# A planned kernel on one core: the planner's prices for turns between tile modes, 110 priorities and the lateness of one state update are changed

## The chip, the core and the metric

The kernel runs on 1 core of one Trainium2 chip. The metric is the device time of a run in microseconds (us); smaller is better. An engine is named as the profile names it where its lines are quoted: PE is TensorE, DVE VectorE, ACT ScalarE, POOL GpSimd, SP the engine that issues most DMAs here.

## What is computed

Two steps follow each other. The first is a gated linear attention, a recurrence over 768 tokens for each of 4 x 8 (batch, head) pairs of width 48:

```python
for t in range(S):
    state = alpha[:, :, t, :, None] * state + einsum('bhd,bhe->bhde', k[:, :, t], v[:, :, t])
    y[:, :, t] = einsum('bhd,bhde->bhe', q[:, :, t], state)
```

The second takes y as 3072 tokens of 384 features through two dense layers with a squared ReLU between them:

```python
h = x @ w_in            # 384 -> 2048, "first layer"
r = maximum(h, 0.0)
return (r * r) @ w_out  # 2048 -> 384, "second layer"
```

All inputs are float32; the kernel multiplies in bfloat16 and adds up in float32.

## The kernel before

**Units.** The work is cut into 12 units of 256 tokens of one batch entry (`units`, line 359; first the first 256 tokens of each of the 4 entries, so units 0 to 3 start a sequence, 4 to 7 continue it, 8 to 11 end it). For a unit there are

- four loads of 384 KB (`ld` a, k, q, v for alpha, k, q, v; `load`, line 494). The loads of unit 2 are issued by GpSimd, all others by SP;
- a front part (`front`, `decays_by_pair`): products of pairs of alphas (`pr`), logarithms (`ln`, `lm`), sums of them on TensorE (`m1i`, `m1s`, the decay sums), exponentials (`ei`, `ea`, `es`, `ec`), then k and q times those (`ekm`, `eqm0`, `eqm1`, lines 687 and 692). From unit 3 on, two DMA transposes (`tr0`, `tr1`, line 703) put the products into the layout for the scores; before that TensorE transposes;
- scores (`p0`, line 881), 32 matmuls on 64x64 tiles into the PSUM tensors psX and psZ, and two masks on VectorE (`mk0` reads psX, `mk1` psZ, line 892) that copy them to SBUF;
- the output (`y`, lines 773 and 784, or 813 and 820), matmuls on 64-row tiles into psX, with the matmuls of the next unit's state update (`kv`, line 752, into psZ) within it from unit 2 on. For units 0 to 2 the update's matmuls are an operation of their own. `sa`, `sc`, `sd` (lines 847 to 858) finish the state on VectorE or GpSimd;
- the eviction of the output (`xe`), its transposition (`xt`, by TensorE at line 927 up to unit 3, by DMA at line 933 after), and for TensorE's a copy (`xv`);
- the first layer in 8 pieces `s1_unit_piece` of 6 matmuls each (line 983), each evicted with a ReLU (`re`, ScalarE line 991 or VectorE line 993) and squared (`sq`);
- the second layer in 8 pieces `s2_unit_half_piece` of 4 matmuls (line 1018), evicted by `oe`, and one store (`out`, line 1034).

The weights are loaded in halves by GpSimd (`win0`, `win1`, `wout0`, `wout1`, line 480).

**The planner.** No order is written out by hand. Every operation is added with an engine (some with a choice of two or three), an assumed cost, a priority and its dependencies (`add`, line 58). `schedule` (line 101) then plays the whole program through with the assumed costs: whenever an engine is free, it takes the ready operation of the smallest priority number. What comes out is a fixed order for each engine (and the engine of each operation with a choice); `place` and `emit` turn dependencies into semaphore waits. So the assumed costs take no time on the chip; they only shape the order. An operation of TensorE has a mode: F for full 128x128 tiles (both layers, decay sums, transposes), T for the scores' 64x64 tiles, R and C for the outputs and updates. A change of mode is called a turn here. `schedule` charges 95 ns for a turn (`SWITCH`, line 45), and stays in a mode while an operation of that mode is ready whose priority number is at most 2500 above the best (`AFFINITY`, line 185).

Priorities come from the unit's number and tables at the head of the kernel function (`FRONT`, `ATTN`, `DENSE`). `LATE_STATE` names units whose state update is added with 4300 instead of 2300 on its priority (line 839), and whose mask of psZ is put before that of psX (line 890).

Until the first weights are there, TensorE is kept busy by matmuls on zeros (`fill`, line 213, called at line 1068).

Of the kernel before, what the change touches and what calls it, by code (L numbers as in the profile page):

```python
# [14 lines left out]
class Op:  # L15
# [5 lines left out]
    def __init__(self, alts, prio, name):  # L21
        self.alts, self.prio, self.name = alts, prio, name
        self.eng = self.fn = self.cost = None
        self.deps = {}
        self.lag = 0
        self.sem = None
        self.users = []
        self.pos = None
        self.mode = ("F", "F")
        self.ready = 0.0  # L30
        self.start = self.end = self.land = None


class Program:
# [7 lines left out]
    SBUF_ONLY = ("pr", "bk", "aq", "ekm", "eqm", "sq", "sb", "sd")  # L42
    BIAS = {"pool": 300}
    DMA_LAST = 800
    SWITCH = 95
    HALVED = {"qks": 3, "kqt": 3, "raw": 3, "ek": 3, "eq": 3, "acm": 2, "laf": 2}
    AFFINITY = 2500

    def __init__(self, nc):
        self.nc = nc  # L50
# [7 lines left out]
    def add(self, eng, fn, cost, prio, reads=(), writes=(), name="", dma=None, lag=0, after=(), mode=("F", "F"),  # L58
            alts=None):

        reads, writes = ([h for k in keys for h in ((k + (0,), k + (1,)) if len(k) == self.HALVED.get(k[0]) else (k,))]
                         for keys in (reads, writes))
        choices = {eng: (fn, cost)}
        if alts:
            choices.update(alts)
        op = Op(choices, prio, name)
        op.idx = len(self.ops)
        op.lag = lag
        op.mode = mode
        if dma is not None:  # L70
            if dma not in self.dma_sems:
                self.dma_sems[dma] = self.nc.alloc_semaphore("d_" + dma)
                self.dma_count[dma] = 0
            self.dma_count[dma] += 1
            op.sem = (dma, self.dma_count[dma])
        for o in after:
            op.deps[o] = True
        for k in reads:
            w = self.writer.get(k)
            if w is not None:  # L80
                op.deps[w] = True
            if k[0] == "ps":
                for r in self.readers.get(k, ()):
                    op.deps.setdefault(r, False)
        for k in writes:
            w = self.writer.get(k)
            if w is not None:
                op.deps[w] = True
            for r in self.readers.get(k, ()):
                if r is not op:  # L90
                    op.deps.setdefault(r, False)
        for k in reads:
            self.readers.setdefault(k, []).append(op)
        for k in writes:
            self.writer[k] = op
            self.readers[k] = []
        op.deps.pop(op, None)
        self.ops.append(op)
        return op

    def schedule(self):
# [8 lines left out]
        mode = "F"  # L110
# [6 lines left out]
        def push(t, kind, what):  # L117
            heapq.heappush(events, (t, next(seq), kind, what))
# [40 lines left out]
        avail = {e: [] for e in engines}  # L159
        order = {e: [] for e in engines}  # L160
        while events:
            now = events[0][0]
            while events and events[0][0] <= now + 1e-9:
                _, _, kind, op = heapq.heappop(events)
                if kind == "tick":
                    if op == clock[1]:
                        advance(now)
                elif kind == "arrive":
                    advance(now)
                    rings[op.eng].append(op)  # L170
                    left[op] = op.lag
                    advance(now)
                elif kind == "ready":
                    best = None
                    for e, (_, c) in op.alts.items():
                        t = max(now, free[e]) + c + self.BIAS.get(e, 0)
                        t += sum(o.alts[e][1] for o in avail[e] if (o.prio, o.idx) < (op.prio, op.idx))
                        if best is None or t < best[0]:
                            best = (t, e)
                    avail[best[1]].append(op)  # L180
            for e in engines:
                while avail[e] and free[e] <= now + 1e-9:
                    o = min(avail[e], key=lambda o: (o.prio, o.idx))
                    if e == "pe" and o.mode[0] != mode:
                        same = [x for x in avail[e] if x.mode[0] == mode and x.prio <= o.prio + self.AFFINITY]
                        if same:
                            o = min(same, key=lambda o: (o.prio, o.idx))
                    avail[e].remove(o)
                    o.eng = e
                    o.fn, o.cost = o.alts[e]  # L190
                    o.start = now
                    o.end = now + o.cost
                    if e == "pe":
                        if o.mode[0] != mode:
                            o.end += self.SWITCH
                        mode = o.mode[1]
                    if e == "pool" or e == "dve" and o.name.startswith(self.SBUF_ONLY):
                        other = shared["dve" if e == "pool" else "pool"]
                        o.end += max(0.0, min(other - now, 1200.0)) * (0.8 if e == "dve" else 0.5)
                        shared[e] = o.end  # L200
                    free[e] = o.end
                    o.pos = len(order[e])
                    order[e].append(o)
                    if o.sem is not None:
                        push(o.end + self.DMA_FIRST[e], "arrive", o)
                    else:
                        land(o, o.end + (self.PE_LATENCY if e == "pe" else 0))
                    push(free[e], "free", None)
# [130 lines left out]
def bass_gla_recurrent__then__act_relu_squared_kernel(  # L339
# [13 lines left out]
    T = 256  # L353
# [12 lines left out]
    RATIO = 4  # L366
    NRAW, NQKS, NKQT, NPM, NV, NXT, NGT, NRR, NOSB = 4, 3, 3, 2, 4, 4, 2, 4, 2
    WS = 2
    LATE_STATE = (1, 2)
    ROW_TILED = tuple(range(PE_TRANSPOSED, G))  # L370
    BY_HEADS = (0,)
    LAST_CUT = 272
# [48 lines left out]
    def table(act):  # L421
# [3 lines left out]
        return None  # L425

    add("act", table, 1300, -1e6, name="table")

    def fill(buf, val):
# [32 lines left out]
    def bcast(t, row, dims):  # L462
        return bass.AP(tensor=t, offset=0, ap=[[row, 128]] + dims)
# [367 lines left out]
    def state(g, alone=True):  # L831
# [5 lines left out]
        if alone:  # L837
            run, cost, reads, writes = state_mm(g)
            add("pe", run, cost, p0 + (4300 if g in LATE_STATE else 2300), reads=reads, writes=writes, name=f"kv{g}", mode=("R", "R"))
        own = bcast(OWN, H, [[1, H], [0, D]])  # L840
# [19 lines left out]
    def scores(g):  # L860
# [24 lines left out]
        for hfs in ((0,), (1,)) if g in BY_HEADS else ((0, 1),):  # L885
# [3 lines left out]
                mode=("T", "T"))  # L889
        for at, hf in enumerate((1, 0) if g in LATE_STATE else (0, 1)):  # L890
            psT, key = halves[hf]
# [208 lines left out]
```

## Time and profile before

| what | us |
|---|---|
| median of 3 runs (lowest, highest) | 176.63 (176.28, 177.08) |
| span of the profiled execution, first to last instruction | 174.5 |
| TensorE busy | 167.6 (96%) |
| VectorE busy | 121.7 (70%) |
| ScalarE busy | 118.9 (68%) |
| GpSimd busy | 15.3 (9%) |

The page gives the profiled execution by its span alone; the 2.1 us between span and median lie before the first and behind the last instruction. The granted TensorE clock is full throughout. The largest groups on TensorE are the first layer (576 matmuls of 256 columns at line 983, busy 73.6) and the second (368 of 384 columns at line 1018, busy 69.4). Matmuls overlap, so busy times of single matmuls add up to more than the time that passes; where pieces are compared below, the time from the start of one to the start of the next is used. A line of the timeline gives the start, the length, the engine, the source line, the operation with its output and inputs, how many were merged, and in brackets how long the engine stood idle before and what ended that. "PEld" is TensorE's loading of weights, beside its matmuls.

### The profile page before, as it was taken

What the parts mean: (1) busy time and instruction counts of PE and PEld (TensorE: products, weight loads), DVE (VectorE), ACT (ScalarE), POOL (GpSimd) and SP (SyncE); (2) the same over time, 40 slices, a digit from 0 to 9 for tenths busy, and PEclk for the clock granted to TensorE, in tenths of its full rate; (3) what the DMA queues carried; (4) which work ended last, traced back from release to release, by engine and by line L of the source; (5) the groups of instructions that cost most, each with busy time, mean ns of one, the idle gap of its engine ahead of it and who ended that gap; (6) DMA issues with size and microseconds to landing.
All of it is one profiled execution on the core that took longest, in us unless ns stands there. A gap on an engine that the chain in (4) does not pass through costs nothing.

```text
span 174.5 us, 5086 instructions
## 1 busy us (share of the span) xinstructions
PE 167.6 (96%) x2233; PEld 129.9 (74%) x2235; DVE 121.7 (70%) x201; ACT 118.9 (68%) x211; POOL 15.3 (9%) x24
## 2 busy tenths in 40 slices
PE   7998988999999989999999999999999999999994
PEld 2566887856787669778778878878788797688773
DVE  5597959596958599978869958958769726322230
ACT  3863689777769669578679759669578564566440
POOL 3160840020002002000200000000000000000000
PEclk9999999999999999999999999999999999999999
DMA  5999999989999899899999998899999690040022
GB/s 144 324 296 197 259 307 214 236 213 313 210 226 174 215 232 190 209 246 193 258 199 183 258 193 207 225 191 264 248 186 209 112 187 4 0 135 4 10 80 90
DMA packets 74742, 33.36 MB, mean 191 GB/s; under 512 B 71648, under 2 KB 71904, under 8 KB 74720
## 3 DMA queue, kind: packets, MB, share of 16 engines
q1 hardware_dynamic: 73184, 28.32, 72.3%
q0 software_dynamic: 1536, 4.72, 12.2%
q8 instruction: 17, 0.28, 0.7%
q14 instruction: 5, 0.04, 0.1%
HBM read 25.17 MB, written 4.72 MB: 171 GB/s over the span
## 4 chain that ended last, share of the span: by engine, by line
PE 62%; DMA 27%; SPq 4%; DVE 2%; ACT 2%; POOL 1%; issue 1%
PE psWH L983 27%; PE psO L1018 26%; DMA win<-in_moe_w_in_dram 7%; DMA raw<-in_q_dram 7%; DMA raw<-in_alpha_dram 5%; DMA wout<-in_moe_w_out_dram 4%; DMA raw<-in_v_dram 4%; SPq L509 3%; PE psX L784 2%; PE psX L773 2%; PE psX L953 2%; PE psX L881 1%; PE psZ L752 1%; DVE pm L892 1%; PE psZ L881 1%
## 5 line engine op out<-in xcount | busy, mean ns | idle before, releaser
L983 PE MATMUL psWH<-xt,win 128*128 128x256 bf16 x576 | 73.6, 274 | 1.5 <-DMA win<-in_moe_w_in_dram 1.0
L983 PEld LDWEIGHTS psWH<-xt,win 128*128 128x128 bf16 x576 | 65.2, 145 | 6.5 <-issue 0.8
L1018 PE MATMUL psO<-wout,gt 128*128 128x384 bf16 x368 | 69.4, 326 | 0.1
L991 ACT ACTIVATE rr<-psWH 128x512 bf16<-128x512 f32 x80 | 47.3, 595 | 23.0 <-PE psWH L983 21.4
L1018 PEld LDWEIGHTS psO<-wout,gt 128*128 128x128 bf16 x368 | 34.7, 98 | 18.2 <-ACT osb L1025 0.3
L1001 DVE TENSOR_TENSOR gt<-rr 128x1024 bf16<-128x1024 bf16 (+1 forms) x43 | 25.6, 597 | 24.7 <-ACT rr L991 24.4
L892 DVE TENSOR_TENSOR pm<-psX,caus 128x1024 bf16<-128x1024 f32 x12 | 14.6, 1218 | 0.9 <-PE psZ L881 0.9
L892 DVE TENSOR_TENSOR pm<-psZ,caus 128x1024 bf16<-128x1024 f32 x12 | 14.6, 1218 | 0.8 <-PE psZ L881 0.8
L1005 ACT ACTIVATE gt<-rr 128x512 bf16<-128x512 bf16 (+1 forms) x17 | 14.1, 828 | 0.5
L912 ACT ACTIVATE xbf<-psX 128x768 bf16<-128x768 f32 x12 | 9.7, 810 | 6.4 <-PE psX L773 5.4
L1025 ACT ACTIVATE osb<-psO 128x384 f32<-128x384 f32 x19 | 9.3, 492 | 5.7 <-PE psO L1018 5.1
L993 DVE TENSOR_SCALAR rr<-psWH 128x512 bf16<-128x512 f32 x16 | 11.0, 688 | 1.6 <-PE psWH L983 0.8
L687 DVE TENSOR_TENSOR qks<-raw,eq 128x384 bf16<-128x384 f32 x18 | 10.0, 589 | 2.4 <-DMA raw<-in_q_dram 2.4
L683 ACT ACTIVATE vbf<-raw 128x768 bf16<-128x768 f32 x10 | 8.4, 841 | 3.6 <-DMA raw<-in_v_dram 3.5
L1068 PE MATMUL psO<-zero 128*128 128x512 bf16 (+1 forms) x33 | 9.3, 417 | 1.4 <-DVE zero L430 1.3
L692 DVE TENSOR_TENSOR qks<-raw,ek 128x768 bf16<-128x768 f32 x11 | 10.4, 950 | 0.0
L847 DVE TENSOR_TENSOR smd<-psZ,sbd 128x384 bf16<-128x384 f32 x8 | 4.5, 557 | 5.3 <-PE psX L773 5.3
L1068 PEld LDWEIGHTS psO<-zero 128*128 128x128 bf16 x35 | 3.4, 108 | 4.9 <-issue 1.9
L658 ACT ACTIVATE la<-raw 128x384 f32<-128x384 f32 x8 | 4.2, 522 | 4.3 <-DMA raw<-in_alpha_dram 4.3
L645 DVE TENSOR_TENSOR ek<-ek,raw 128x384 f32<-128x384 f32 x10 | 5.6, 557 | 1.2 <-ACT ek L636 1.1
L636 ACT ACTIVATE ek<-psWH 128x384 f32<-128x384 f32 x10 | 4.9, 490 | 1.4 <-PE psWH L628 1.4
L619 ACT ACTIVATE lab<-prd 128x384 bf16<-128x384 f32 x10 | 5.2, 520 | 0.7 <-DVE prd L616 0.6
(115 smaller groups left out, 156.8 us busy)
## 6 DMA issues: line engine op xcount, KB each, us to landing
raw<-in_alpha_dram SPq DMA_DIRECT2D x11, 384.0 KB, 3.6
raw<-in_k_dram SPq DMA_DIRECT2D x11, 384.0 KB, 4.4
raw<-in_q_dram SPq DMA_DIRECT2D x11, 384.0 KB, 4.0
raw<-in_v_dram SPq DMA_DIRECT2D x11, 384.0 KB, 4.8
out_dram<-osb SPq DMA_DIRECT2D x11, 384.0 KB, 4.0
win<-in_moe_w_in_dram POOLq DMA_DIRECT2D x2, 768.0 KB, 10.0
wout<-in_moe_w_out_dram POOLq DMA_DIRECT2D x2, 768.0 KB, 8.4
raw<-in_alpha_dram POOLq DMA_DIRECT2D x1, 384.0 KB, 5.5
```

The lines of the kernel that those rows point to most:

```text
L687: add("dve", lambda e, j=j, dst=dst: e.tensor_tensor(dst, RAW[r][:, 2, :, j, :].rearrange("p (n x) d -> p n x d", x=2), EQ[la][:, j].rearr ...
L692: add("dve", lambda e, a=a, E=E: e.tensor_tensor(QKS[qs][:, a, :, :, 0:D], RAW[r][:, 1 + a].rearrange("p h j d -> p j h d"), E[la][:].rear ...
L892: add("dve", lambda e, hf=hf, psT=psT: e.tensor_tensor(PM[pm][:, hf].rearrange("p r n j t -> p (r n) (j t)"), psT[:, :, :].rearrange("p r ...
L912: add("act", lambda e: e.activation(XBF[x2][:], psX[:, :, 0:HD], AF.Copy), act_ns(2 * HD), p0 + 6100, reads=[("ps", "X", 0), ("ps", "X", 1 ...
L983: ins = pe.matmul(psH[hb][:, i * T:(i + 1) * T], WIN[:, kk, hidden(fj)], mov, start=(kk == 0), stop=(kk == KT - 1))
L991: add("act", lambda e, hb=hb, rr=rr: e.activation(rr, psH[hb], AF.Relu), act_ns(512), pu + 600, reads=[("ps", "H", hb)], writes=[("rr", rb ...
L993: alts={"dve": (lambda e, hb=hb, rr=rr: e.tensor_scalar(rr, psH[hb], 0.0, None, ALU.max), dve_ns(512))})
L1001: add("dve", lambda e, dst=dst, sq=sq: e.tensor_tensor(dst, sq, sq, ALU.mult), 148 + k * 267, pu + 1200, reads=[("rr", rb, h) for h in ran ...
L1005: "act": (lambda e, dst=dst, sq=sq: e.activation(dst, sq, AF.Square), act_ns(k * 512))})
L1018: ins = pe.matmul(psS, GT[gt][:, fj, j, :], WOUT[:, fj, :], start=(fj == 0), stop=(fj == FT - 1))
L1025: add("act", lambda e, j=j, psS=psS: e.activation(OSB[ob][:, j], psS, AF.Copy), act_ns(DM), ps_ + 700, reads=[keyS], writes=[("osb", ob, j ...
L1068: pr.fill(lambda n: lambda pe: pe.matmul(psO[:, 0:n], ZERO[:, 0:128], ZERO[:, 0:n], skip_group_check=True), ((512, 216, 420), (256, 109, 2 ...
```

## The change

It has three parts, all in the planner's numbers:

1. A turn is charged by its kind: 112 ns from scores (T) to full tiles, 100 ns from outputs (R) to full tiles, 95 otherwise. A first-layer piece right behind a turn is charged 57 ns more, and where the best operation behind a turn would be a first-layer piece, a ready full-tile operation that is none is taken instead, if its priority number is at most 2500 above (`WARM`).
2. A table adds a number of its own to the priorities of 110 operations (`DELTA`).
3. `LATE_STATE` is cut from units 1 and 2 to unit 1.

```diff
-    SWITCH = 95
+    SWITCH = {("T", "F"): 112, ("R", "F"): 100}
+    COLD_S1 = 57
+    DELTA = {
+       "s2_11_1_1": 332203, "s1_11_3": -23664, "y11": -65523, "ldv11": 132157, "s2_9_1_3": 59450, "s2_9_0_3": 88014,
...
     AFFINITY = 2500
+    WARM = 2500
...
+        prio += self.DELTA.get(name, 0)
...
                         same = [x for x in avail[e] if x.mode[0] == mode and x.prio <= o.prio + self.AFFINITY]
+                        if not same and o.name.startswith("s1_"):
+                            same = [x for x in avail[e] if x.mode[0] == "F" and not x.name.startswith("s1_")
+                                    and x.prio <= o.prio + self.WARM]
...
-                            o.end += self.SWITCH
+                            o.end += self.SWITCH.get((mode, o.mode[0]), 95)
+                            if o.name.startswith("s1_"):
+                                o.end += self.COLD_S1
...
-    LATE_STATE = (1, 2)
+    LATE_STATE = (1,)
```

Every computing instruction of the kernel is still there, apart from the matmuls on zeros at the start (34 instead of 35 of them); what differs is the order on each engine, and for some operations the engine. What the planner makes of it, as far as the text below speaks of it:

- **TensorE.** 26 turns to full tiles in both. In 13 of them a first-layer piece came next, in 11 a second-layer piece; now 8 and 16. The scores of units 5, 6 and 7 have fewer dense pieces ahead of them. Unit 2, before and after:

```
before: tr1_2 s1_1_4 s1_1_7 p0_2 s1_1_6 s2_0_0_2 s2_0_0_3 kv2 s2_0_1_0 m1i3 s2_0_1_1 s2_0_1_2 s2_0_1_3 m1s3 y2
after:  tr1_2 s1_1_5 s2_0_0_0 s2_0_0_1 p0_2 s1_1_6 s1_1_7 s2_0_0_2 kv2 s2_0_0_3 m1i3 s2_0_1_0 s2_0_1_1 m1s3 s2_0_1_2 s2_0_1_3 y2
```

  Unit 3, behind its output: `y3 s2_2_0_1 s2_2_0_2 xt3 s2_2_0_3 s1_3_0` becomes `y3 s2_2_0_0 s2_2_0_1 xt3 s2_2_0_2 s2_2_0_3 s1_3_0`.
- **VectorE.** `mk0_2` comes before `mk1_2`. `pr3` goes there from GpSimd and stands behind `mk1_2`; `xe3` goes there from ScalarE. `sd4` leaves, so unit 4's masks follow `eqm0_5` and `eqm1_5` directly.
- **GpSimd.** `pr2 pr3 pr5 sd5 vc7` become `pr2 vc2 vc4 sd4 pr6 vc7 sd7 vc9 vc11` (`vc` is the copy of v to bfloat16). The loads of unit 2 go a, k, v, q instead of a, k, q, v.
- **SP.** The loads of units 3 and 4 go a, q, v, k instead of a, k, q, v. Unit 5's q and v go ahead of the store of unit 1 instead of behind it, and from unit 4 on the DMA transposes of x go ahead of a store instead of behind it; other stores stand one or two loads further back too.

More of the change, by code (lines that the diff above doesn't have):

```diff
@@ L44 @@
     DMA_LAST = 800
-    SWITCH = 95
+    SWITCH = {("T", "F"): 112, ("R", "F"): 100}
+    COLD_S1 = 57
+    DELTA = {
[19 rows of a table added]
+    }
     HALVED = {"qks": 3, "kqt": 3, "raw": 3, "ek": 3, "eq": 3, "acm": 2, "laf": 2}
     AFFINITY = 2500
+    WARM = 2500
     def __init__(self, nc):
```

18 rows, old and new, of the table DELTA are left out of this document.

## The prediction

> **What bounds the kernel now.** I read the stretches of the span first, then TensorE's timeline with its waits, then the chain of waits, then VectorE and GpSimd where the chain leads.
>
> The stretches (length; busy time and instructions of each engine; granted clock; DMA share; GB/s):
>
> ```profile
> 17.50:41.00 23.50, 21.81 (x274) 17.35 (x274) 19.02 (x29) 18.75 (x33) 6.73 (x8) 1.00 1.01 249
> 41.00:66.00 25.00, 24.15 (x392) 18.52 (x389) 19.12 (x31) 18.07 (x36) 1.00 (x1) 1.00 1.03 222
> 66.00:140.00 74.00, 74.00 (x1005) 59.03 (x1005) 59.74 (x92) 55.33 (x98) 2.31 (x2) 1.00 0.99 210
> ```
>
> From 66 to 140 us TensorE (first column) is busy 74.00 of 74.00 at clock 1.00: nothing is to be had there but cheaper pieces. Between 17.5 us, where the first piece of the first layer starts, and 66 us it stands still 1.69 + 0.85 = 2.54 us. DMA is full too, at 0.99 to 1.03, up to 140 us. That is the stage in which an edit of order can win or lose.
>
> TensorE's timeline shows the price of a turn and two of the stops:
>
> ```profile
> 58.47 0.88 PE L983 MATMUL psWH<-xt,win 128*128 128x256 bf16 x6 [0.25 <-ACT xt L941]
> ...
> 62.46 1.47 PE L983 MATMUL psWH<-xt,win 128*128 128x256 bf16 x12
> 64.53 0.19 PE L773 MATMUL psX<-sbd,kqt 64*128 64x48 bf16 x1 [0.60 <-DVE pm L892]
> ...
> 65.58 1.53 PE L983 MATMUL psWH<-xt,win 128*128 128x256 bf16 x12
> ```
>
> Twelve first-layer matmuls take 1.47 us, but 1.53 right behind the 64-row tiles of an output: 0.06 more. The chain of waits says where the 0.60 comes from:
>
> ```profile
> 54.29 0.95 ACT gt L1005
> 55.25 0.18 SPq L1034
> 55.42 0.04 issue
> 55.47 5.22 DMA raw<-in_q_dram
> 60.69 0.02 issue
> 60.71 1.03 DVE qks L687 x2
> 61.74 0.47 DVE sbd L858
> 62.21 2.28 DVE pm L892 x2
> 64.49 0.05 issue
> 64.53 0.27 PE psX L773 x8
> ```
>
> A load of q is issued behind a store (L1034), lands 5.22 us later, and VectorE then has two products, a state update and two masks in its queue before the output can start.
>
> **The parts.** The sum is made against the profiled execution, whose page gives a span of 174.5 us; the median of the three runs is 176.63, so 2.1 us lie around the span, and I carry differences over to the median. Stops are counted start to start: the time from one piece to the next, less what the same piece takes elsewhere. So 0.60 shown becomes 0.67, since the pipeline's tail hides some.
>
> *Turns: -0.23.* The planner now knows different prices, but the chip sees only an order. Both orders have 26 turns back to full tiles: 13 go to the first layer, 11 to the second and 2 elsewhere before, 8, 16 and 2 after. A first-layer piece behind a turn is 0.057 longer (0.712 against 0.655 start to start), a second-layer piece 0.011 (0.661 against 0.650). 5 x 0.046 = 0.23. The turn itself costs the same 0.095 into every mode.
>
> *Unit 4's output: -0.67.* On SP the load of q for unit 5 goes ahead of unit 1's store: it is issued 55.47 - 54.24 = 1.23 us earlier. The state update that stood between the products and the masks (0.47) goes to GpSimd. The masks end 1.7 us earlier, at 62.8; TensorE, 1.0 earlier by the rest of this sum, comes at about 62.9 (64.53 - 0.67 - 1.0). That is just covered, so the far end of this term is -0.3.
>
> *Unit 3's transposes: -0.42.* Before, one second-layer piece (0.65) lies between the transposes of x and the first layer of unit 3, which waits for the copy (58.47, start to start 0.42 late). After, there are two: 0.65 of cover for 0.42, spare 0.23. The eviction of x in front of them goes from ScalarE (0.81) to VectorE, where no such row stands; the nearest, a product over 768, took 0.95, so 0.14 of cover goes as well. Ends: -0.42 and 0.
>
> *Small stops: -0.2.* From 53.7 us on, five waits of 0.04 to 0.12 for evictions add up to 0.3. After, most of these pieces stand one or two places further from the eviction that they wait for; I take two thirds as gone. Ends: -0.3 and 0.
>
> *Unit 2's update, no longer late: +0.2.* Its masks swap. TensorE's part of the update writes psZ, which the psZ mask must have read by then. Before, that mask is first:
>
> ```profile
> 34.45 1.22 DVE L892 TENSOR_TENSOR pm<-psZ,caus 128x1024 bf16<-128x1024 f32 x1
> 35.59 1.22 DVE L892 TENSOR_TENSOR pm<-psX,caus 128x1024 bf16<-128x1024 f32 x1
> 37.00 0.56 DVE L850 TENSOR_TENSOR smd<-psZ,own 128x384 bf16<-128x384 f32 x1 [0.19 <-PE psZ L752]
> ```
>
> After, it is second and ends 0.69 + 1.14 + 1.22 = 3.05 us after the scores begin; TensorE is there after the scores (0.57), a first-layer piece behind a turn (0.71), another (0.65) and a second-layer piece with the turn (0.75): 2.68. A new stop of 0.4. Behind it in TensorE's queue stand a second-layer piece and the decay sums of unit 3, which wait besides for a product now queued on VectorE behind this mask instead of alone on GpSimd. The scores start 0.66 earlier, since one first-layer piece fewer lies ahead, and an old stop of 0.2 in front of unit 2's transposes loses its cause. So the decay sums come at 37.7, as before (37.75). Up to unit 2's output both orders do the same work; before it stopped 0.5 there for unit 3's k product (ended 40.66), and after it has little left to stop for, but new small ones ahead of it. I take 0.2 later; ends -0.3 (the stop of 0.5 goes, half is used up) and +0.9 (both stops of 0.4 and 0.5 in full).
>
> *Loads of units 3 and 4: 0.* k is now loaded last of the four. By the landings in the trace it comes where v came, at 38.85 instead of 36.38. VectorE reads k at 39.71: 0.9 of cover. If k lands later than that, unit 2's output waits one for one.
>
> *Work moved to GpSimd: 0.* Behind unit 0, five of the units' operations ran there before, nine after. VectorE's row beside one of them:
>
> ```profile
> 85.67 1.65 DVE L687 TENSOR_TENSOR qks<-raw,eq 128x384 bf16<-128x384 f32 x2
> ```
>
> Two products took 1.65 here and 1.03 at 60.71; in between GpSimd cast v (85.82, 1.08 us). So an operation on GpSimd holds VectorE up by 0 to 0.62. VectorE is busy 59.74 of 74.00, so its queue hides that; if it falls on the products ahead of a mask it is at most 0.6. The Trainium skill, SBUF — State Buffer, section SBUF: two separate sides, says that the two engines share a pair of ports under an exclusive lock, so that the loser blocks for the whole instruction; the row agrees with its 0.62. By that rule four more such operations would hold VectorE up by 2.5 us in all (4 x 0.62, an estimate); the sum would then be 178.1 if all of it fell in front of TensorE.
>
> *Thin covers: +0.3.* New covers of 0.1 to 0.3 stand at unit 4's output, at the first layer of unit 3 and at unit 2's output. I take one of them as broken by its full size; ends 0 and +0.9.
>
> Sum: -0.23 - 0.67 - 0.42 - 0.2 + 0.2 + 0.3 = -1.02, so 176.63 - 1.02 = **175.6 us** (-0.6%). All first ends: about -1.9, 174.7. All last ends: +1.3, 177.9. The front (the first weights land at 17.45, and six operations of TensorE lie before the second half in both) and the tail behind the last piece are the same.
>
> **Rivals.** *Transposes bind: 176.1 to 176.5.* Later units' scores wait for two DMA transposes. By the trace's landings they came at 68.85, 81.02 and 92.72 for units 5, 6 and 7, and the scores started at 70.61, 83.83 and 95.71. The new order puts 1.30, 1.91 and 1.96 us less TensorE work ahead of these scores. With the gain of 1.0 they come at 68.3, 80.9 and 92.75. If the transposes keep their times, unit 5 waits 0.55 and the gain shrinks to about 0.5; a further 0.4 gone by instruction fetches or stores gives no change. For it: DMA share 0.99. Against it: q is issued a store earlier in unit 5, and from unit 4 on the transposes of x go ahead of the stores.
>
> *Slower: 177.7.* The same place, but the transposes come later than before: with DMA full, GpSimd holding VectorE (0.6) ahead of the products of unit 5 or 7 makes SP's in-order queue issue them late, and everything behind them. It decides from 1.6 us late (unit 5 landing after 70.4): then the wait eats the whole gain; at 2.6 late the kernel is 1.05 slower. Before, a landing was late by about 1.9 at single places (q of unit 5 at 58.8 to 60.7), so it is possible.
>
> *The turns are all it does: 176.4.* The stops reappear elsewhere at the same size, and 0.23 is left: no change by measure.
>
> *More: 174.8.* All stops go and no thin cover breaks.
>
> **How the numbers follow.** Forecast 0.45, at 175.0 to 175.75 by itself; more, 0.08; transposes bind or turns alone, 0.28; slower, 0.19. The runs spread from 176.28 to 177.08, so 0.5% (0.9 us) is what can be told from no change. Faster 0.53, within 0.5% 0.28, slower 0.19. The range 174.9 to 177.5 leaves out most of "more" and the far part of "slower".
>
> **What would show it.** Right: no stop of TensorE for pm near 63 us nor for xt near 58 us; one of about 0.4 for pm at 36 us; from 66 to 140 us still 74.00 busy; twelve first-layer matmuls of 1.53 rarer. Wrong: TensorE waiting for kqt transposes between 66 and 100 us, or for k at 41 us; VectorE products stretched beside GpSimd in front of a mask that TensorE waits for.

## The result, and the profile after

The changed kernel takes 178.20 us in the median of 22 runs (176.74 to 180.38); the kernel before, run beside it on the same chip, 177.01 (175.45 to 182.14). The ratio is 1.0076, with a 95% interval of 1.0050 to 1.0101: slower, where 175.6 us and faster was forecast. In all ratios of this document runs over 1.5% above the fastest of their kernel are left out, which for the kernel before takes away up to 16 of 29 runs, so that a ratio can lie above 1 where the median, which is over all runs, lies below that of before (e3, e4). The profiled execution of after took 179.54 us, with a span of 177.8, 3.3 more than that of before; it lies 1.3 above after's median, so sizes are also read from a second profile of the same kernel below.

The same three stretches as for before (length; busy time and instructions of PE, PEld, DVE, ACT, POOL; granted clock; DMA share; GB/s), now of after:

```profile
17.50:41.00 23.50, 22.52 (x296) 17.39 (x286) 20.10 (x30) 17.36 (x32) 6.71 (x8) 1.00 1.03 252
41.00:66.00 25.00, 22.85 (x349) 17.53 (x346) 19.25 (x30) 18.32 (x35) 3.53 (x3) 1.00 1.01 218
66.00:140.00 74.00, 71.84 (x1012) 57.81 (x1004) 56.34 (x86) 53.31 (x99) 3.68 (x4) 1.00 0.98 206
```

The first stretch gained (22.52 of TensorE busy, 21.81 before): there before waited 0.67 us for the second half of the first layer's weights, which landed at 22.27, and at 21.30 in after, and the other gaps add up to about the same in both (1.02 and 0.98). The second lost 1.30, and the third, which had no gap at all before, lost 2.16. The clock is 1.00 and the DMA share about 1 in both kernels, but the bytes per second of the third stretch fell from 210 to 206: DMA is as busy and moves less.

What TensorE waited for from 40 to 140 us (engine, line, releaser: total, times, longest), before:

```profile
PE psX L773 <- DVE pm L892: 0.6, 1, 0.6
PE psX L813 <- DVE qks L692: 0.4, 1, 0.4
PE psWH L983 <- ACT xt L941: 0.3, 1, 0.3
```

and after (lines are 29 higher):

```profile
PE psWH L654 <- ACT lab L648: 2.2, 2, 1.6
PE psX L802 <- ACT vbf L712: 1.1, 1, 1.1
PE psX L910 <- DVE ek L674: 0.5, 1, 0.5
PE psO L1047 <- DVE osb L1056: 0.4, 1, 0.4
PE psX L802 <- POOL vbf L711: 0.3, 1, 0.3
```

None of the three old rows is left, as forecast: no wait for a mask near 63 us, none for the copy of x near 58. The new rows sum to 4.5 us against 1.3, and all lead back to a load or a DMA transpose. `lab` is the logarithm of unit 4's and unit 5's alpha, which waits for the load of alpha; `vbf` is the cast of v of units 10 and 7, which starts when v lands. For the scores of unit 7 the row names a VectorE product, which ended at 96.07; but unit 7's second transpose landed at 96.11, and the scores started at 96.20, 0.09 later (in the second profile, e1 below, 95.23 and 95.32). The row with `osb` is an eviction that stands on VectorE behind unit 7's product of alphas, which waited until 80.28 for a load. These lines stand behind the six stops, in order of time:

```profile
44.16 0.34 PE L654 MATMUL psWH<-lab,linc 128*128 128x384 bf16 x1 [1.60 <-ACT lab L648]
...
54.70 0.34 PE L654 MATMUL psWH<-lab,linc 128*128 128x384 bf16 x1 [0.55 <-ACT lab L648]
...
81.83 0.82 PE L1047 MATMUL psO<-wout,gt 128*128 128x384 bf16 x4 [0.37 <-DVE osb L1056]
...
91.02 0.18 PE L802 MATMUL psX<-sbd,kqt 64*128 64x48 bf16 x1 [0.27 <-POOL vbf L711]
...
96.20 0.42 PE L910 MATMUL psX<-kqt 64*64 64x128 bf16 x16 [0.47 <-DVE ek L674]
...
129.38 0.19 PE L802 MATMUL psX<-sbd,kqt 64*128 64x48 bf16 x1 [1.05 <-ACT vbf L712]
```

The landings behind these rows, taken from the trace's DMA records (issue > landing, us):

| transfer | before | after | after, second profile |
|---|---|---|---|
| alpha of unit 5 | 47.98 > 52.66 | 48.07 > 53.50 | 46.42 > 51.58 |
| alpha of unit 7 | 72.88 > 76.17 | 73.52 > 80.26 | 72.76 > 78.51 |
| v of unit 7 | 81.15 > 85.76 | 83.16 > 90.00 | 82.02 > 89.08 |
| second transpose of unit 7 | 88.62 > 92.72 | 91.11 > 96.11 | 90.28 > 95.23 |
| v of unit 10 | 119.23 > 124.95 | 121.39 > 128.46 | 121.15 > 128.13 |

The queue that issues them, SP in after, around unit 7 (start, length of the issue, line; L732 transposes k and q, L962 x, L538 loads, L1063 stores):

```profile
78.22 2.30 SPq L732 DMA_TRANSPOSE kqt<-qks  x1
80.57 1.29 SPq L962 DMA_TRANSPOSE xt<-xbf  x1
81.91 0.58 SPq L538 DMA_DIRECT2D raw<-in_q_dram  x1
82.54 0.58 SPq L1063 DMA_DIRECT2D out_dram<-osb  x1
83.16 0.43 SPq L538 DMA_DIRECT2D raw<-in_v_dram  x1
```

SP works in order, and up to 83.6 without a pause. The store of unit 3 now stands between q and v of unit 7; v is issued right behind it, while the store is in flight (82.54 to 87.56), and takes 6.84 us instead of 4.61. In before v stood behind the same store too, but with q between them:

```profile
80.05 0.58 SPq L1034 DMA_DIRECT2D out_dram<-osb  x1
80.68 0.43 SPq L509 DMA_DIRECT2D raw<-in_q_dram  x1
81.15 0.88 SPq L509 DMA_DIRECT2D raw<-in_v_dram  x1
```

So of the 4.24 us by which v lands later, 2.01 are there when it is issued, and 2.23 come in flight. The chain of waits of after (start, length, what) ends there:

```profile
83.16 6.84 DMA raw<-in_v_dram
90.00 0.05 issue
90.05 0.83 POOL vbf L711
...
91.02 0.27 PE psX L802 x8
```

TensorE takes unit 6's output at 91.02, when the cast of unit 7's v is done, because unit 7's update is taken within it.

The stops counted start to start, as in the prediction, sum to 3.85 us before and 7.28 after: 3.43 more, less 0.23 for the turns, makes 3.20 of the 3.3 by which the spans differ.

### The profile page after: what moved, and what is told of

Read it like the earlier page. It is cut to its first block, busy times and chain, and to the rows that moved or that the text cites. A ratio compares the mean times of both kernels' runs of the same rounds, so it can differ in the third digit from the quotient of the medians.

```text
span 177.8 us, 5089 instructions
## 1 busy us (share of the span) xinstructions
PE 168.4 (95%) x2232; PEld 130.6 (73%) x2234; DVE 121.1 (68%) x196; ACT 118.1 (66%) x213; POOL 19.0 (11%) x27
## 4 chain that ended last, share of the span: by engine, by line
PE 51%; DMA 36%; DVE 3%; SPq 3%; POOL 2%; ACT 2%; issue 1%
PE psO L1047 22%; PE psWH L1012 20%; DMA raw<-in_alpha_dram 13%; DMA raw<-in_v_dram 8%; DMA raw<-in_q_dram 6%; DMA wout<-in_moe_w_out_dram 5%; DMA win<-in_moe_w_in_dram 5%; SPq L538 2%; POOL raw L538 2%; PE psX L813 2%; PE psX L802 2%; PE psX L982 1%; PE psZ L781 1%; PE psX L910 1%; ACT rr L1020 1%
## 5 line engine op out<-in xcount | busy, mean ns | idle before, releaser
L1047 PE MATMUL psO<-wout,gt 128*128 128x384 bf16 x368 | 70.3, 327 | 0.4 <-DVE osb L1056 0.4
L1020 ACT ACTIVATE rr<-psWH 128x512 bf16<-128x512 f32 x86 | 50.9, 596 | 23.5 <-PE psWH L1012 22.0
L1047 PEld LDWEIGHTS psO<-wout,gt 128*128 128x128 bf16 x368 | 34.0, 98 | 18.6 <-DVE osb L1056 0.6
L711 POOL CAST vbf<-raw 128x768 bf16<-128x768 f32 x5 | 5.1, 1023 | 86.6 <-DMA raw<-in_v_dram 86.6
L716 DVE TENSOR_TENSOR qks<-raw,eq 128x384 bf16<-128x384 f32 x18 | 11.3, 654 | 0.0
L941 ACT ACTIVATE xbf<-psX 128x768 bf16<-128x768 f32 x9 | 7.3, 808 | 5.1 <-PE psX L802 4.8
L645 DVE TENSOR_TENSOR prd<-raw 128x384 f32<-128x384 f32 x8 | 4.4, 555 | 8.2 <-DMA raw<-in_alpha_dram 8.2
L674 DVE TENSOR_TENSOR ek<-ek,raw 128x384 f32<-128x384 f32 x10 | 6.3, 627 | 2.9 <-ACT ek L665 2.9
L1022 DVE TENSOR_SCALAR rr<-psWH 128x512 bf16<-128x512 f32 x10 | 6.8, 685 | 1.3 <-PE psWH L1012 1.2
L712 ACT ACTIVATE vbf<-raw 128x768 bf16<-128x768 f32 x6 | 5.0, 837 | 1.5 <-DMA raw<-in_v_dram 1.5
```

Of the source, the lines that this page charges most:

```text
L716: add("dve", lambda e, j=j, dst=dst: e.tensor_tensor(dst, RAW[r][:, 2, :, j, :].rearrange("p (n x) d -> p n x d", x=2), EQ[la][:, j].rearr ...
L941: add("act", lambda e: e.activation(XBF[x2][:], psX[:, :, 0:HD], AF.Copy), act_ns(2 * HD), p0 + 6100, reads=[("ps", "X", 0), ("ps", "X", 1 ...
L1020: add("act", lambda e, hb=hb, rr=rr: e.activation(rr, psH[hb], AF.Relu), act_ns(512), pu + 600, reads=[("ps", "H", hb)], writes=[("rr", rb ...
L1047: ins = pe.matmul(psS, GT[gt][:, fj, j, :], WOUT[:, fj, :], start=(fj == 0), stop=(fj == FT - 1))
```

## The experiments

In the kernels with an edited order the order of every engine is written out as a list, taken from what the planner made of before or of after, and edited as shown. Their line numbers are 67 higher than after's, or 68 higher than before's. Experiments that shared the runs of the kernel before stand in groups of four; e9 to e12 ran on another chip than the rest:

| run | median (lowest to highest) | before, beside it | ratio to before, 95% interval |
|---|---|---|---|
| e1 after again | 180.04 (177.97 to 181.44) | 179.59 | 1.0095, 1.0047 to 1.0144 |
| e2 after, SP order of before | 184.10 (182.69 to 187.31) | 179.59 | 1.0308, 1.0240 to 1.0376 |
| e3 before, SP order of after | 178.70 (177.67 to 180.58) | 179.59 | 1.0043, 0.9999 to 1.0087 |
| e4 after, less on GpSimd | 178.94 (177.91 to 181.43) | 179.59 | 1.0065, 1.0017 to 1.0114 |
| e5 after, loads mended | 177.83 (175.88 to 180.82) | 178.96 | 0.9939, 0.9881 to 0.9997 |
| e6 e5, and decay sums later | 177.98 (176.56 to 181.37) | 178.96 | 0.9987, 0.9940 to 1.0033 |
| e7 before, contiguous loads | 175.58 (175.23 to 176.09) | 178.96 | 0.9890, 0.9829 to 0.9951 |
| e8 after, contiguous loads | 174.61 (174.28 to 175.32) | 178.96 | 0.9838, 0.9776 to 0.9899 |
| e9 before again | 178.83 (176.99 to 181.28) | 179.27 | 1.0017, 0.9975 to 1.0059 |
| e10 e5, and unit 2 as before | 179.93 (176.67 to 181.09) | 179.27 | none taken |
| e11 e8, and unit 2 as before | 175.43 (174.69 to 175.74) | 179.27 | 0.9810, 0.9760 to 0.9859 |
| e12 e8, less on GpSimd | 175.16 (174.76 to 175.96) | 179.27 | 0.9810, 0.9760 to 0.9859 |
| e13 e11 mended | 174.07 (173.52 to 174.72) | 178.78 | 0.9778, 0.9726 to 0.9830 |
| e14 e10 mended | 177.73 (175.62 to 180.44) | 178.78 | 0.9965, 0.9919 to 1.0011 |
| e15 before, two edits | 179.10 (175.66 to 182.25) | 178.78 | none taken |
| e16 e7, the same two edits | 175.76 (175.31 to 176.29) | 178.78 | 0.9875, 0.9818 to 0.9931 |

The first theory after the result was that SP's new order brings the loads late; the rivals, that the new order of the computing asks for them sooner than a full DMA can bring them, and that GpSimd holds VectorE up.

**e1: after, unchanged.**

> The changed kernel once more, for an undisturbed profile and a ratio beside the other runs. The median of its runs was 178.2 against 177.0 (ratio 1.0076). If the stops seen in its first profile (for unit 4's alpha 1.77, unit 5's 0.71, at unit 9's output 1.12) are its own, a second profile shows TensorE waiting at the same three places; if they were chance of one execution, they stand elsewhere and add up to a like sum. Ratio 1.005 to 1.010 either way.

Of the stops, those for alpha of unit 5 (0.55; 0.71 in the first profile), v of unit 7 (1.17; 0.34), the transposes of unit 7 (0.58; 0.54) and v of unit 10 (1.59; 1.12) came again; the largest of the first profile, 1.77 for alpha of unit 4, did not (that alpha landed at 40.97, 42.97 in the first profile), nor does it in e4, e5 and e6, so it was chance. The other places belong to the order, the sizes change from run to run.

**e2 and e3: the SP orders exchanged.** Each keeps the computing engines of its name and takes SP's list from the other kernel, e2:

```diff
-... lda3 ldq3 ldv3 ldk3 ... ldq5 ldv5 out1_1 lda6 ldk6 tr0_5 tr1_5 xt4 ldq6 ldv6 out2_1 ldk7 lda7 ...
+... lda3 ldk3 ldq3 ldv3 ... out1_1 ldq5 ldv5 lda6 ldk6 tr0_5 tr1_5 out2_1 xt4 ldq6 ldv6 lda7 ldk7 ...
```

> The changed kernel's orders on the four computing engines, but SP issues its loads, transposes and stores in the order of before. Theory 1, the order of the loads is at fault (k last in units 3 and 4, stores moved): the late loads vanish, ratio 0.994 (the forecast gain). Theory 2, the computing order asks for loaded data before a full DMA can bring it, whatever SP's order: ratio 1.005 to 1.012, TensorE still stops for alpha of units 4 and 5. Theory 3, GpSimd holds VectorE up: ratio 1.005 to 1.01, stops at scores and outputs stay.

> The orders of before on the computing engines, but SP's order of after. Theory 1: ratio 1.01 or more, with stops for k of unit 3 or alpha of unit 4. Theory 2: within 0.3% of before, or 0.5% faster, since unit 5's q lands a store earlier and the stop of 0.67 at unit 4's output goes. Theory 3: as theory 2.

With before's SP order after is worse, not better; its third stretch, in a profile of one of its two longest runs (span 185.5):

```profile
66.00:140.00 74.00, 68.15 (x957) 53.15 (x954) 53.45 (x81) 49.96 (x91) 4.02 (x4) 1.00 0.93 197
```

5.85 us of TensorE's time are gone there. So SP's new order as a whole helps the new computing order, and the first theory falls. In e3 the stop at unit 4's output is gone (q of unit 5 earlier, as forecast), and others come: 0.82 and 0.22 us for alpha of unit 7, which landed at 77.63 behind k instead of 76.17 ahead of it, 0.68 at unit 9's output. In the profile, then, single places of SP's order do harm; in time e3 is not told from before (median 0.9 us lower, ratio 1.0043 with 0.9999 to 1.0087).

**e4: less work on GpSimd.** Casts of v of units 2, 4, 7, 9, 11 go to ScalarE, `sd4`, `sd7` and `pr6` to VectorE:

```diff
-pool: ... wout0 pr2 wout1 vc2 vc4 sd4 pr6 vc7 sd7 vc9 vc11
+pool: ... wout0 pr2 wout1
```

> The changed kernel with eight of its nine later GpSimd operations moved: the five casts of v to ScalarE, two state updates and one product of alphas to VectorE, each put in its queue where GpSimd would have started it. All other orders are those of after. Theory 3 (GpSimd's operations stretch VectorE's two-input ones by up to 0.62 and so delay the transposes): ratio back to 0.995 to 1.00, k and q products at 0.56 and 0.95 everywhere. Theories 1 and 2: 1.005 to 1.01 as after.

Its median is 1.1 us below e1's, but the intervals of the ratios overlap, and the stops for v of units 7 and 10 stay (0.81 and 2.16 us). Left open here; e12 settles it for loads that are not late.

**e5 and e6: single places of SP's order.**

```diff
-... ldk7 lda7 ... ldq7 out3_1 ldv7 ... ldq9 out5_1 ldv9 ldk10 lda10 ... ldq10 out6_1 ldv10 ...
+... lda7 ldk7 ... ldq7 ldv7 out3_1 ... ldq9 ldv9 out5_1 lda10 ldk10 ... ldq10 ldv10 out6_1 ...
 (e6 too, on TensorE)
-... m1i5 s2_1_1_2 s2_1_1_3 y3 ...
+... s2_1_1_2 s2_1_1_3 y3 m1i5 ...
```

> The order on every engine is that of after, but for SP: v of units 7, 9 and 10 goes ahead of the store that stands before it in after, and alpha of units 7 and 10 ahead of k. Theory 'late loads' (after's order of work needs v of units 7 and 10 sooner, and its SP order brings it later, behind a store): the stops in front of the outputs of units 6 and 9 (0.34 to 1.17 and 1.12 to 1.59 us) go, the others stay: 1.5 to 2.5 us below after, a ratio to before of 0.995 to 1.000. Rival 'any order of a full DMA' (what is taken from v is paid by the next transfer): the two stops go, others of the same size come behind them (transposes of units 7 and 10 or alpha of 8 and 11), the time stays within 0.5 us of after. Rival 'GpSimd' (casts of v on GpSimd are the cause): no change at the outputs.

> As the kernel before this one in the call, and TensorE takes the decay sums of unit 5 three operations later, behind the output of unit 3. Theory 'late loads': the stop of 0.55 to 0.71 us for the logarithm of unit 5's alpha goes too, another 0.5 us less, if unit 5's transposes, which follow from these sums, still land in time; ratio to before 0.992 to 0.998. Rival 'any order of a full DMA': unit 5's transposes go out later by about 1 us and its scores wait as much; no gain.

e5 is below before, ratio 0.9939, a little more than the theory of late loads had given (0.995 to 1.000). But its profile (span 179.1, the longest of its twelve runs) has not lost the waits; from 40 to 140 us:

```profile
PE psX L869 <- DVE pm L988: 1.9, 2, 1.3
PE psWH L721 <- ACT lab L715: 1.0, 2, 0.7
PE psX L977 <- DVE la L756: 0.9, 1, 0.9
PE psX L977 <- DMA kqt<-qks: 0.9, 1, 0.9
```

The cast of v is gone from the rows, and masks stand in its place: q of unit 7, with v now right behind it in place of the store, took 5.8 us (82.08 to 87.88; 4.5 in after, 3.9 in before), and the products and masks came late with it. In e6 the stop at the decay sums of unit 5 is gone, and 1.27 at unit 3's output, 0.89 at its transposes and 0.90 at the scores of unit 7 stand there. In the profiles, then, the rival, that a full DMA takes back what one transfer is given, holds for a good part. In time e5 gained more than it allows (by the medians 1.1 us below before, where after was 0.5 and 1.2 above); e6 is not told from before.

**e7 and e8: the same orders, a lighter DMA.** All loads read contiguous pieces; other values than the unit's own are loaded, the same in both kernels:

```diff
-src = t[b, :, t0:t0 + T, :].rearrange("h (p j) d -> p h (j d)", j=2)
+src = t.rearrange("b h s d -> (b h s d)")[int(g) * 98304:(int(g) + 1) * 98304].rearrange("(p n) -> p n", p=128)
-dst = dst.rearrange("p h j d -> p h (j d)")
+dst = dst.rearrange("p h j d -> p (h j d)")
```

> The orders of before, but each load of alpha, k, q and v reads one contiguous piece of 384 KB as 128 packets of 3072 bytes instead of 1024 packets of 384 bytes; the values that are loaded are others than the unit's own, and nothing else is changed. It is the yardstick for the next kernel. All theories: DMA share falls well below 0.99 between 66 and 140 us; of before's stops (3.85 us) those that go back to a load (0.67 at unit 4's output, 0.5 at unit 2's) go: 1 to 2 us below before, ratio 0.988 to 0.995.

> The orders of after with the same contiguous loads. Theory 'late loads' (after's order of work is as good as forecast, and only the full DMA turns it into waits): no stop at unit 5's decay sums nor at the outputs of units 6 and 9; 0.2 to 1.0 us below the kernel of before with contiguous loads, since the turns (0.23) and the stops of before that come from its order remain as gains. Rival 'the order of work' (the stops come from engines, GpSimd's hold on VectorE or shorter covers): 0.8 to 1.5 us above it, as after stands to before.

This decides. The packets, after and e8:

```profile
DMA packets 74742, 33.36 MB, mean 188 GB/s; under 512 B 71648, under 2 KB 71904, under 8 KB 74720
```

```profile
DMA packets 35190, 33.36 MB, mean 193 GB/s; under 512 B 26592, under 2 KB 26848, under 8 KB 35168
```

e8's second and third stretch:

```profile
41.00:66.00 25.00, 25.00 (x412) 20.03 (x407) 20.63 (x32) 20.01 (x38) 3.31 (x3) 1.00 0.89 197
66.00:140.00 74.00, 74.00 (x1033) 59.51 (x1031) 57.73 (x86) 54.79 (x100) 3.85 (x4) 1.00 0.90 206
```

With the same bytes in half the packets the DMA share falls to 0.9, TensorE has no gap from 41 to 140 us, and the list of its waits from 40 us on is empty. After is now faster than before: 174.61 against 175.58, ratio 0.9947 (0.9921 to 0.9973, worked out from the six runs of each). The 0.97 us between the medians are near the forecast's 1.02, but that the totals agree is in part luck: the forecast's largest term, 0.67 at unit 4's output, is not in them, since e7 has lost that stop too, and neither are its +0.2 and +0.3. Both kernels gain by the lighter DMA, before 3.4 us, after 3.6 against its first runs and 5.4 against e1. The Trainium skill, Perfetto Trace Analysis, section DMA Optimizations, says that DMAs under 2 KB carry a significant overhead per transfer; the runs agree, by 1.1% (0.9890) for before. The rival, that the new order waits for engines, would have left after 0.8 to 1.5 us behind, and falls.

**e9: before, unchanged.**

> The kernel of before, unchanged, for a second profile of it. In its first profile TensorE stood still for 3.85 us between 17.5 us and the end, none of it in 66 to 140 us, and it took 176.6 us; later runs of it go from 175.4 to 183.8. Theory 'late loads': its slower runs lose at single places to loads and DMA transposes as well, so that the profile shows stops behind transfers in 66 to 140 us as many us as its time lies above 176.6. Rival 'only the new order is thin': the stops stay as in the first profile, and the difference lies in the front, in the tail or in the clock.

The span is 176.3, 1.8 above the first profile. Two thirds of it arise in front: the first layer starts 0.51 later, and the second layer waits for its weights:

```profile
31.82 1.47 PE L1018 MATMUL psO<-wout,gt 128*128 128x384 bf16 x8 [1.09 <-DMA wout<-in_moe_w_out_dram]
```

From 66 to 140 us 0.20 of TensorE's busy time are lost, nearly all at 131 to 133 us (0.54 start to start):

```profile
66.00:140.00 74.00, 73.80 (x1034) 59.07 (x1027) 58.64 (x92) 55.44 (x99) 2.06 (x2) 1.00 0.97 209
```

The rival had the place, the front, and the other theory the cause, a late transfer. This one slower run of before is late mostly at the weights; from 66 to 140 us its order keeps nearly its full cover.

**e10, e11, e13, e14: unit 2.** e10 (with the loads of e5) and e11 (with contiguous loads):

```diff
-dve:  ... mk0_2 mk1_2 sq1_7 pr3 sa2 ...       pool: ... wout1 vc2 vc4 ...
+dve:  ... mk1_2 mk0_2 sq1_7 sa2 ...           pool: ... wout1 pr3 vc2 vc4 ...
```

> after with v of units 7, 9 and 10 ahead of the store and alpha of 7 and 10 ahead of k, and besides the order of before at unit 2: the mask of psZ ahead of that of psX, and unit 3's product of alphas on GpSimd again. Meant as the version that beats both. Theory: the two stops at unit 2's update and the decay sums behind it (0.42 and 0.56 us in every profile of after) go, without a new one at unit 2's output: 0.7 us below the kernel with the loads mended alone, ratio to before 0.988 to 0.998. Rival 'full DMA': what is gained at 36 us is lost again to loads, since they start no sooner: ratio 0.995 to 1.003.

> after with contiguous loads (other values than the unit's own are loaded) and the order of before at unit 2 alone: mask of psZ first, unit 3's product of alphas on GpSimd. Theory 'a stop costs what it lasts': the stops of 0.42 and 0.56 us go and nothing takes their place, 0.6 to 1.0 us below after with contiguous loads (174.6), about 173.8. Rival 'unit 2's output is bound by unit 3's k product anyway', as in before, where TensorE waited 0.50 us for it: 0 to 0.3 us below.

e11 came out 0.8 us above e8 instead of 0.6 to 1.0 below, by a slip of mine that is the lesson of this case in small. GpSimd in e11:

```profile
35.10 0.99 POOL L714 TENSOR_TENSOR prd<-raw 128x384 f32<-128x384 f32 x1 [10.10 <-DMA raw<-in_alpha_dram]
36.05 1.01 POOL L778 CAST vbf<-raw 128x768 bf16<-128x768 f32 x1
```

and TensorE behind it:

```profile
37.11 0.52 PE L848 MATMUL psZ<-vbf,qks 64*128 64x96 bf16 x16 [1.83 <-POOL vbf L778]
```

I had put the product of alphas, which waits for a load until 35.10, ahead of a cast whose v had landed long before. TensorE waited 1.83 us for the cast. e10 has the same slip (2.49 us start to start at unit 2's update) and tells nothing else. e13 (contiguous loads) and e14 (with the loads of e5) have `vc2 pr3 vc4`:

> after with contiguous loads (other values than the unit's own are loaded) and the order of before at unit 2: mask of psZ first, unit 3's product of alphas on GpSimd, now behind the cast of unit 2's v (ahead of it, it made that cast wait for alpha of unit 3, and TensorE 1.9 us for the cast). Theory 'a stop costs what it lasts': the stops of 0.42 and 0.56 us go, nothing takes their place: 0.6 to 1.0 us below after with contiguous loads (span 172.9). Rival 'unit 2's output is bound by unit 3's k product': 0 to 0.3 us below, with a stop at that output.

> The same order at unit 2 with the kernel's own loads, and SP's order mended (v of units 7, 9 and 10 ahead of the store, alpha of 7 and 10 ahead of k). Theory: no stop at 36 to 38 us, loads of units 3 and 4 as late as before: ratio to before 0.988 to 0.998. Rival 'full DMA': ratio 0.995 to 1.003, with stops at the scores or outputs of units 6 to 9.

e13: 174.07, 0.54 below e8 (ratio 0.9963, 0.9934 to 0.9992, though from another group of runs); in the profiles unit 2's output comes at 40.12 instead of 40.78, and all that follows 0.66 earlier. The stop at the update is gone, that at the decay sums stayed (0.49). By the profiles this is just within what the theory gave (0.6 to 1.0), by the medians just short of it. e14, with the kernel's own loads, is 0.9965 (0.9919 to 1.0011) of before: the version meant to beat both is below before by its median (177.73 against 178.78), but not beyond doubt, in the range of both forecasts, and no better than e5. It has no stop at unit 2's update, and still 0.67 at the decay sums of unit 5, 0.96 for unit 7's transposes and 1.35 for a mask at unit 9's output.

**e12: GpSimd without late loads.** The edit of e4 on e8.

> after with contiguous loads (other values than the unit's own are loaded), and eight of the nine operations that run on GpSimd behind unit 0 moved off it, casts of v to ScalarE, two state updates and a product of alphas to VectorE. It asks what GpSimd's work costs when loads are not late. Theory 'GpSimd is hidden': within 0.3 us of after with contiguous loads (174.6). Rival 'GpSimd holds VectorE up' by the 1.85 us by which the products beside it are longer: 0.5 to 1.5 us below.

The product of q (engine, shapes, count; busy, mean ns), e8 and e12:

```profile
L783 DVE TENSOR_TENSOR qks<-raw,eq 128x384 bf16<-128x384 f32 x18 | 10.7, 620 | 0.2 <-DMA raw<-in_q_dram 0.2
```

```profile
L783 DVE TENSOR_TENSOR qks<-raw,eq 128x384 bf16<-128x384 f32 x18 | 9.4, 553 | 0.0
```

GpSimd did hold VectorE up, by 67 ns in the mean of these 18, and without it nothing is won: from unit 2's output to the last piece 128.89 us against 128.86. (The median is 0.55 above e8's, from another chip; in the profiles 0.38 arise ahead of unit 2's output, where TensorE waits 0.66 instead of 0.08 at decay sums near 27 us.) VectorE is busy 57.73 of the 74.00 us of e8's third stretch, so its queue has room. The Trainium skill's lock (SBUF — State Buffer, section SBUF: two separate sides) shows in the length of the products and not in the time. So the prediction's aside, 178.1 by that rule, came near the measured time by another cause, as far as the stops show one.

**e15 and e16: two edits alone, on before.** q and v of unit 5 ahead of `out1_1` on SP, and on TensorE:

```diff
-... xt3 s2_2_0_3 s1_3_0 s2_2_1_0 p0_4 ...
+... xt3 s2_2_0_3 s2_2_1_0 s1_3_0 p0_4 ...
```

> before with two edits of the change alone: q and v of unit 5 ahead of the store of unit 1 on SP, and on TensorE one more second-layer piece between the transposes of x of unit 3 and that unit's first layer. Theory 'late loads' (the change was right where it took a stop away, and wrong where it brought work forward against the loads): the stops of 0.67 at unit 4's output and of 0.42 at unit 3's first layer go, and 66 to 140 us stays as in before: ratio 0.992 to 0.997, and below after. Rival 'full DMA': the transfers of unit 5 come earlier at the cost of the next ones: ratio 0.998 to 1.003.

> The two edits with contiguous loads (other values than the unit's own are loaded). There the stop at unit 4's output is gone already without the edit, so only the 0.42 of unit 3 can be won: theory 'a stop costs what it lasts': 0.3 to 0.5 us below before with contiguous loads (span 173.8). Rival: the copy of x, which the first layer waits for, is not what ends the wait, and nothing is won.

A miss. The piece that I put in as cover waits itself; TensorE in e16:

```profile
58.73 0.82 PE L1086 MATMUL psO<-wout,gt 128*128 128x384 bf16 x4 [0.63 <-ACT osb L1093]
```

Start to start it stands 0.80 for an eviction, where 0.42 for the copy of x were to be saved: 175.76, no gain on e7. The changed kernel covers the copy with two pieces of the half before, and neither waits in its profile. In e15 the stop at unit 4's output went, as expected, but TensorE waited 1.12 and 0.59 us for weights near 18 and 31 us, and a transposition of x was late by 1.82 us at 124.5; its six runs do not tell it from before.

## Why the prediction was wrong

The step that failed is "Thin covers: +0.3" (ends 0 and +0.9), with the zero for the loads, which was worked out for units 3 and 4 alone. In its place stand the stops for loads and transposes: start to start 1.77 + 0.71 (alpha of units 4 and 5), 0.53 (the eviction behind alpha of unit 7), 0.34 + 1.12 (v of units 7 and 10) and 0.54 (transposes of unit 7), 5.0 us in the first profile; 4.2 in e1 (alpha of unit 5 0.55, the eviction 0.31, v 1.17 + 1.59, transposes 0.58). The sum without the term is -1.02 - 0.3 = -1.32; with 5.0 it is +3.7 and with 4.2 +2.9, beside measured differences of the spans of +3.3 and +3.0. The medians differ by less, 1.2 us: before's profile is of a short run with few late transfers (about 176.3 us, where its groups of runs have medians up to 179.6), and after's is of a long one. Every run whose span is on record took 1.7 to 1.8 us more than its span, so the 2.1 us that the text took to lie around the span were 0.3 too many, the difference between two runs of before.

How I came to it: the text read the DMA share of 0.99 as "the stage in which an edit of order can win or lose", and then took landings out of the trace of before for transfers that the change puts elsewhere in a queue. A landing is a result of the order. The planner lets a unit's loads start when q of the unit before has landed (the gates in the kernel function, line 1046 of before), so one late q passes on to all that follow: q of units 5, 6 and 7 landed at 60.69, 72.86 and 84.58 before, at 59.45, 73.05 and 86.40 after. After leads by 1.24 at unit 5 and is 1.82 behind two units later.

Point by point:

- *Turns, -0.23.* Agrees. From unit 2's output to the last piece e7 takes 129.68 us and e8 128.86: 0.82 less, of which the stops at unit 3 and three small ones (0.42 + 0.06 + 0.04 + 0.04) leave 0.26.
- *Unit 4's output, -0.67.* The stop is gone in after, e1, e3 and e15, where q of unit 5 goes ahead of the store. In e7 it is gone without the edit: q landed at 58.09.
- *Unit 3's transposes, -0.42.* Gone in after and e8.
- *Small stops, -0.2.* Those of 0.04 to 0.12 are gone; e1 has a new one of 0.24 for an eviction near 62 us.
- *Unit 2's update, +0.2.* The new stop is there with 0.24 to 0.42. Behind it the decay sums wait 0.55 more, a wait that the text named without a size; they come at 37.24, where it had 37.7. Both, start to start, in after:

```profile
35.58 0.51 PE L781 MATMUL psZ<-vbf,qks 64*128 64x96 bf16 x16 [0.16 <-DVE pm L921]
...
37.24 0.34 PE L654 MATMUL psWH<-lab,linc 128*128 128x384 bf16 x1 [0.39 <-ACT lab L648]
```

  Since the old stop of 0.50 at unit 2's output is gone, that output comes at 40.59 in after and 40.72 in before: net nothing, within the ends. Put back, it gains 0.66 (e13).
- *Loads of units 3 and 4, 0.* k of unit 3 landed at 39.49, 0.64 later than the text had, and cost nothing. Alpha of unit 4, of which the text said nothing, was issued earlier than before (36.96, 37.75 before) and landed later (42.97, 41.02 before); it cost 1.77 once.
- *GpSimd, 0.* Right where loads are not late (e12); with the kernel's own loads e4 leaves it open.
- *Rivals.* "Slower, 177.7" had the mechanism, a full DMA and SP's in-order queue, and the right sign. Its cause, GpSimd holding VectorE up, won nothing when taken away in e12 and is left open by e4. Its place was unit 5's transposes; these landed 1.34 us later than before, at 70.19, and TensorE, itself late by then, did not wait for them. What it waited for was v right behind a store, alpha (of unit 7, behind k), and unit 7's transposes. "Transposes bind" was right for unit 7. Both together had the place that the text named as proof against it: TensorE waiting for transposes between 66 and 100 us.

What stays open: how much of each late transfer comes from its neighbours in the queue and how much from when the computing frees its buffers. e2 says that the new computing order needs SP's new order; no run parts the two further. Whether GpSimd's hold on VectorE makes late transfers later still is not shown either (e4). Nor is it shown why e15's transposition of x was late.

## What to carry to other kernels

Where DMA is full, a landing read from the trace of before holds only while the queue in front of it stays; an edit that brings computing forward must be charged with the transfers it then waits for, and the covers of all loads on the way are its price list. To see whether an order is good or only short of data, run both orders with the same bytes in larger packets. An instruction that waits for a load is best kept behind everything in its queue that doesn't.

## What was not expected of the hardware

- The kernel before, unchanged, had medians of 176.63 to 179.59 us in its groups of runs, and single runs from 175.45 to 184.22. With contiguous loads the six runs of each kernel lie within 1.3 us, so most of the spread comes with the many small packets. It is there at a granted clock of 1.00 (176.29 to 181.98 us among the runs beside e1); the longest runs, all seven above 182.14, show 0.99.
- From unit 5 on, loads of 384 KB took 3.55 (q of unit 6) to 7.07 us (v of unit 10) from issue to landing in one execution of after, all at a DMA share near 1.
- From 66 to 140 us of after, issuing one DMA transpose kept SP busy for 1.3 to 3.7 us, and a load or a store mostly for 0.4 to 0.6 (up to 1.8).
